# A two-part kernel (complex scan and local attention) on one core: engines of some stores and evictions, and a new recording order

## The chip, the core and the metric

The kernel runs on one core of one Trainium2 chip. The time is the device time of a run in microseconds (us); where several runs are given, the median counts. Engines are named as in the profile: PE (TensorE, matmuls), PEld (its weight loads), DVE (VectorE), ACT (ScalarE), POOL (GpSimd) and SP (SyncE, which here only begins DMAs). SPq and ACTq stand for the issue of DMAs in the queues of SP and ACT.

## The reference

Two independent computations share one output of 1 x 2048 x 896 in bf16: columns 0 to 447 are A's, 448 to 895 are B's. Inputs are bf16, S = 2048, D = 448.

```python
def A(x, Lambda_re, Lambda_im, B_re, B_im, C_re, C_im, log_dt, Dskip):
    Lam = Lambda_re + 1j * Lambda_im                    # 448 complex states
    Lam_bar = exp(exp(log_dt) * Lam)
    Bu = x @ (((Lam_bar - 1) / Lam)[:, None] * (B_re + 1j * B_im)).T
    h[t] = Lam_bar * h[t - 1] + Bu[t]                   # over 2048 steps
    return 2 * real(h @ (C_re + 1j * C_im).T) + x * Dskip

def B(x, wqkv, wo):                                     # 16 heads of 28
    q, k, v = split(x @ wqkv)
    idx = pos[:, None] - 2 * arange(8)                  # 8 earlier places, 2 apart
    logits = sum(q[s] * k[idx[s]]) * 28 ** -0.5, masked where idx < 0
    return (softmax(logits) weighted sum of v[idx]) @ wo
```

## The kernel before

**Units, order, banks.** The kernel does not issue instructions directly. Each piece of work is a unit that is added to a planner (`P.add(engine or engines, estimated cost, function, dependencies, ...)`), 614 in all. Two tables then fix everything: ORDER lists the units in the order in which they are recorded (an entry x stands for unit x % 1000, on the engine number x // 1000 of its choices), and BANKS gives, in that order, the PSUM bank (of 8; most uses take two neighbours) that each accumulation gets. The costs and priorities in `P.add` are not read in a run; they were used when the tables were made. Each engine then runs its own instructions in the recorded order and waits for semaphores where an operand comes from elsewhere. A unit that is recorded earlier may still have to wait in its engine's queue, and what stands behind it on that engine waits with it.

**B.** `loads` transposes B's x by DMA, in quarters of the first half (b = 0, L349) and four pieces of the second half (b = 1, L353), and loads wqkv by groups of columns (L360, L362). `load_v` (L392) is one unit that issues four loads of the v part, wv (L337 to L341). `prep` projects q and k: `first` (PE L494) takes the first 256 columns of b = 0 in quarters, `proj` (PE L453) the rest; kinds K, Q by groups of 128 columns, and kind M for the last 64 columns of both, whose weights are gathered into `wm` by a copy (u_wm, DVE L434). ACT evicts each accumulation to q and k (L202 CAST for k, L204 ACTIVATE for the scaled q). A matmul of 64 partitions (`rr`) runs in a half-row mode of the PE array. `qk` multiplies q with shifted k on DVE (L560, prods; a half product is 128 x 4 x 512) and sums over the head on PE (L573) into logits. `softmax` evicts the logits (ACT L600, L609), sums and normalizes. The attention weights are copied to the layout that `pv` wants (L202 COPY ra, 128 x 512, by ACT or DVE). `v_proj` (PE L673, L682) projects v; `pv` multiplies weights and shifted v on DVE (L727) and adds in a tree (L733 to L744), block by block (b = 0, then b = 1), transposes by DMA (L771) and multiplies with wo on PE (L790, and the half-row L797). Its evictions (`ev2`) and stores (L807) go out in pairs of rows; the last pair is split by row ("tail").

**A.** `setup` makes the powers of Lam_bar: an exponential (ACT L957), two sines (ACT L960, behind a table load), their squares and products on DVE (L987 to L1002), Gd (L1023). A's x is loaded by DMA transposes (L868, on SP's queue), Bcat by evictions of `setup_weights`. `scan` treats the 448 complex states as 896 rows in seven blocks m0 to m6 of 128: input matmuls (L1135), a local scan over 16 steps with powers (`powers`: one block's pw is built by ACT L1082 in single products, or by DVE L1084 in a wide one), evictions on ACT (eP L1148, e L1156, eG L1163, pbuf L1174 and more) and on PE small matmuls on pbuf and pw (L1179, L1185), until h[m] is evicted (L202 CAST h). Three pad buffers go round, so block m + 3 waits for block m's last eviction, and pw goes round in four. `outputs` multiplies h with Ccat on PE (L1319, two rows of 16 at once: 7 blocks for each), with x times D put in by a matmul or by ACT (`seed`, L1331), evicts (L202 CAST ra) and stores (L1342). The last three of the eight pairs are evicted and stored by row; of the very last row ACT evicts 256 columns and DVE 192.

**Queues.** All 20 stores go out from SP's queue; so do wv's loads and nearly all others.

Of the kernel before, what the change touches and what calls it, by code (L numbers as in the profile page):

```python
# [16 lines left out]
D = 448  # L17
# [58 lines left out]
]  # L76
BANKS = [
# [3 lines left out]
]  # L81
# [8 lines left out]
def act(n):  # L90
    return n / 1200.0 + 0.055
# [6 lines left out]
def vec2(n):  # L98
    return n / 1920.0 + 0.07
# [1382 lines left out]
```

## Time and profile before

| | us |
|---|---|
| median of 3 runs | 135.98 (134.9 to 136.2) |
| the profiled execution's own time | 135.03 |
| its span in the profile | 133.3 |
| PE busy | 126.8 (95% of the span) |
| DVE busy | 113.4 (85%) |
| ACT busy | 105.4 (79%) |
| POOL busy | 12.1 (9%) |

The span runs from the first to the last instruction that the profile shows; the run's own time is 1.7 us longer. A row of the timeline gives the start and the length in us, the engine, the line of the kernel, the operation, the tiles written and read, sizes and counts, and in brackets the idle time ahead of it with what ended it. The granted clock of PE was 1.00 in the stages used below.

### The profile page before, as it was taken

How to read it: one execution, taken by the hardware profiler on the slowest of the kernel's cores; microseconds unless marked ns; L12 is line 12 of the kernel's file. 1: busy time of each engine (PE TensorE's matmuls, PEld its weight loads, DVE VectorE, ACT ScalarE, POOL GpSimd, SP SyncE). 2: the span in 40 equal slices, each digit the busy share in tenths (PEclk: the TensorE clock that was granted, in tenths of full speed). 3: DMA queues.
4: the chain of work that ended last, by engine and by line, in shares of the span. 5: the costliest groups of instructions: out<-in, count | busy, mean ns of one | idle time of the engine just before them, and what ended most of it. 6: DMA issues, size and time to landing. Idle time of an engine off the chain costs nothing.

```text
span 133.3 us, 2479 instructions
## 1 busy us (share of the span) xinstructions
PE 126.8 (95%) x921; PEld 63.4 (48%) x921; DVE 113.4 (85%) x130; ACT 105.4 (79%) x189; POOL 12.1 (9%) x28
## 2 busy tenths in 40 slices
PE   6999989999999999999999899999999999999990
PEld 2477333434546434464454255444566555545430
DVE  5256998999999999999999999999999999992011
ACT  2067968987999957879999999989999649569270
POOL 6940491000000000000000000000000000000000
PEclk9999999999999999999999999999999999999998
DMA  4999949989346758827869988006620685318642
GB/s 91 207 199 186 146 100 232 178 193 201 73 91 104 170 147 290 222 51 152 266 97 143 260 210 244 19 0 138 147 67 0 165 227 199 102 63 219 234 148 93
DMA packets 47759, 20.25 MB, mean 152 GB/s; under 512 B 38774, under 2 KB 46346, under 8 KB 47748
## 3 DMA queue, kind: packets, MB, share of 16 engines
q1 hardware_dynamic: 46676, 19.77, 64.7%
q10 hardware_dynamic: 880, 0.31, 1.2%
q8 instruction: 7, 0.11, 0.4%
q0 software_dynamic: 192, 0.03, 0.1%
q14 instruction: 4, 0.03, 0.1%
HBM read 5.18 MB, written 4.19 MB: 70 GB/s over the span
## 4 chain that ended last, share of the span: by engine, by line
PE 73%; ACT 15%; SPq 5%; DMA 3%; issue 1%; DVE 0%; ACTq 0%
PE banks L1319 16%; PE banks L1135 12%; PE banks L453 10%; PE banks L790 7%; PE banks L673 7%; PE banks L573 6%; SPq L349 4%; PE banks L1179 3%; DMA rb<-in_B_wqkv_dram 3%; ACT qk L202 2%; ACT pbuf L1174 2%; PE banks L1152 2%; ACT h L202 2%; PE banks L797 2%; ACT banks L1217 1%; SPq L360 1%
## 5 line engine op out<-in xcount | busy, mean ns | idle before, releaser
L560 DVE TENSOR_TENSOR prods<-qk 128x4096 bf16<-128x4096 bf16 (+1 forms) x18 | 31.7, 1809 | 0.3 <-ACT qk L202 0.2
L1135 PE MATMUL banks<-xaT_sb,Bcat 128*128 128x512 bf16 (+1 forms) x112 | 26.9, 381 | 0.6 <-ACT h L202 0.6
L202 ACT CAST ra<-banks 128x896 bf16<-128x896 f32 (+2 forms) x24 | 17.9, 773 | 7.8 <-PE banks L797 4.2
L202 ACT CAST qk<-banks 128x512 bf16<-128x512 f32 (+3 forms) x20 | 16.9, 843 | 3.9 <-PE banks L453 1.4
L733 DVE TENSOR_TENSOR prods<-prods 128x7168 bf16<-128x7168 bf16 x4 | 15.6, 3892 | 0.1
L727 DVE TENSOR_TENSOR prods<-ra 128x7168 bf16<-128x7168 bf16 x4 | 15.5, 3886 | 0.0
L727 DVE TENSOR_TENSOR prods<-ra,qk 128x7168 bf16<-128x7168 bf16 x4 | 15.5, 3886 | 0.1
L1319 PE MATMUL banks<-Ccat,h 128*128 128x448 bf16 x64 | 14.7, 353 | 0.0
L453 PE MATMUL banks<-rb 128*128 128x512 bf16 (+1 forms) x64 | 13.3, 379 | 0.6 <-ACT sh L960 0.6
L1135 PEld LDWEIGHTS <-Bcat 128*128 128x128 bf16 (+1 forms) x112 | 9.1, 100 | 9.7 <-issue 3.7
L673 PE MATMUL banks<-wv,rb 128*128 128x448 bf16 (+1 forms) x64 | 13.7, 354 | 0.0
L1319 PE MATMUL banks<-Ccat,qk 128*128 128x448 bf16 x48 | 11.7, 352 | 0.0
L790 PE MATMUL banks<-wo_p,rb 128*128 128x448 bf16 x48 | 10.9, 354 | 0.0
L1174 ACT CAST pbuf<-banks 128x64 bf16<-128x64 f32 (+1 forms) x42 | 9.3, 229 | 0.9 <-PE banks L1179 0.6
L1179 PE MATMUL banks<-pbuf,pw 128*128 128x64 bf16 x77 | 9.7, 235 | 0.2
L204 ACT ACTIVATE qk<-banks 128x512 bf16<-128x512 f32 (+2 forms) x10 | 8.4, 849 | 1.2 <-PE banks L453 1.0
L1179 PEld LDWEIGHTS <-pw 128*128 128x128 bf16 x77 | 6.5, 105 | 5.5 <-issue 1.9
L453 PEld LDWEIGHTS <-rb 128*128 128x128 bf16 (+1 forms) x64 | 5.1, 96 | 7.9 <-issue 2.8
L206 DVE CAST ra<-banks 128x192 bf16<-128x192 f32 x2 | 0.7, 358 | 9.2 <-ACT ra L202 9.2
L1319 PEld LDWEIGHTS <-h 128*128 128x128 bf16 x64 | 5.8, 98 | 5.3 <-issue 0.7
L1084 DVE TENSOR_TENSOR pw<-Dm,spair 128x1280 bf16<-128x1280 bf16 (+1 forms) x13 | 8.0, 664 | 0.0
L1148 ACT CAST eP<-banks 128x1024 bf16<-128x1024 f32 x7 | 7.1, 1014 | 0.9 <-PE banks L1135 0.9
(145 smaller groups left out, 201.8 us busy)
## 6 DMA issues: line engine op xcount, KB each, us to landing
out_dram<-ra SPq DMA_DIRECT2D x12, 224.0 KB, 2.3
xaT_sb<-in_A_x_dram SPq DMA_DIRECT2D x2, 448.0 KB, 4.8
out_dram<-ra SPq DMA_DIRECT2D x8, 112.0 KB, 1.7
ra<-ra SPq DMA_DIRECT2D x2, 392.0 KB, 4.1
qk<-qk SPq DMA_DIRECT2D x2, 392.0 KB, 4.1
wv<-in_B_wqkv_dram SPq DMA_DIRECT2D x2, 336.0 KB, 4.2
ra<-ra SPq DMA_DIRECT2D x1, 588.0 KB
qk<-qk SPq DMA_DIRECT2D x1, 588.0 KB, 5.6
```

The source lines that it names most:

```text
L202: nc.scalar.copy(out, in_)
L204: nc.scalar.mul(out, in_, scale)
L453: nc.tensor.matmul(out(e)[:, j0:j1], lhsT=w, rhs=self.xB[rows, b, j0:j1, c, :], start=e not in begun, stop=True, skip_group_check=True)
L560: V.tensor_tensor(p[:, :, a:a + n], q[:, t0 + a:t0 + a + n].unsqueeze(1).to_broadcast([NCH, 4, n]), bass.AP(k.tensor, k.offset, [k.ap[0], ...
L673: nc.tensor.matmul(box["ps"][:, e, 0:D], lhsT=self.xB[rows, b, jj, c, :], rhs=self.wv[rows, c, :], start=e not in begun, stop=True, skip_g ...
L727: V.tensor_tensor(out.rearrange("p (u i d h) -> p u i d h", u=4, i=4, d=DH), self.attn[b][:, r].rearrange("p (x u i) h -> p x u i h", x=2, ...
L733: V.tensor_tensor(T1, T1, T2, op=ALU.add)
L790: nc.tensor.matmul(ps, lhsT=o[:, kt + x, :], rhs=self.wo_p[:, (KT + 1) * x + kt, :], start=(kt == 0), stop=False, skip_group_check=True)
L1135: mt(ps(i), lhsT=lhsT, rhs=rhs, start=i not in begun, stop=True, **kw)
L1174: nc.scalar.copy(pb[:, dst, PAD:PAD + NCH // d], tot(a, d))
L1179: mt(tot(out, 2), lhsT=L(T * unit * k), rhs=pb[:, src, PAD - sh:PAD - sh + NCH // 2], start=False, stop=True, **kw)
L1319: nc.tensor.matmul(ps, lhsT=self.h[m][:, i, g * NCH:(g + 1) * NCH], rhs=self.Ccat[:, m, :], start=False, stop=(m == NM - 1), skip_group_ch ...
```

## The change

Six things change; all but the fourth come from the tables or are allowed by them.

1. Every store unit may be begun by SP or by ACT. In the new table 19 of 20 stay on SP; the very last store (unit 611) is begun by ACT.
2. `load_v` (unit 134), which already had the choice, is now begun by ACT: `1134`.
3. The copy of wm may be done by DVE or ACT. The table leaves it on DVE.
4. The last row of A's and of B's output is evicted whole by one engine (448 columns, on ACT), where ACT did 256 and DVE 192; two units fewer. The last row of a pair no longer depends on the store of the first.
5. One of the attention copies of the first block moves from ACT to DVE (`1192`). The small powers of block m2 move from DVE to ACT (`344`, `1344`), those of m3 from ACT to DVE (`1378`, `378`).
6. ORDER and BANKS are new throughout. At the end of PE's queue B's last pair of rows was done for both rows together (12 matmuls L790, then 4 half-row ones L797), with two rows of A's output (14 matmuls L1319) behind it; now it is done row by row (6 and 2, twice) and one row of A's output (7 matmuls) is behind it.

```diff
--- before.py
+++ after.py
@@ -44,40 +44,39 @@
 ORDER = [
-    22, 2, 5, 0, 1, 6, 23, 7, 1017, 4, 8, 3, 9, 39, 15, 41, 16, 40, 18, 44, 46, 43, 42, 45, 24, 25, 27, 28, 10,
...
-    210, 171, 1378, 146, 212, 178, 114, 176, 213, 133, 179, 169, 282, 207, 206, 283, 208, 209, 190, 314, 284,
...
-    613,
+    4, 2, 3, 0, 5, 1, 41, 39, 15, 16, 42, 6, 7, 22, 40, 43, 45, 44, 46, 59, 23, 24, 47, 57, 1017, 18, 60, 58,
...
+    154, 157, 98, 86, 97, 130, 163, 99, 125, 84, 165, 120, 108, 122, 111, 1134, 88, 162, 158, 159, 310, 100, 33,
...
+    311, 283, 285, 286, 209, 210, 211, 287, 288, 213, 316, 313, 549, 289, 290, 312, 291, 1192, 292, 314, 318,
...
+    539, 543, 542, 544, 590, 594, 595, 596, 579, 608, 609, 607, 597, 540, 541, 545, 546, 547, 548, 610, 1611,
 ]
 BANKS = [
...
...
 ]
@@ -431,8 +430,8 @@
         self.u_proj = []
         lim = PRI["lim"]
         sc = DH ** -0.5
-        self.u_wm = P.add("DVE", vec2(896), lambda: nc.vector.tensor_copy(
-            self.wm[:], self.wqk.rearrange("p k (a c) -> p k a c", a=2)[:, :, :, DF:D]),
+        self.u_wm = P.add(("DVE", "ACT"), (vec2(896), act(896) + 0.05), lambda eng: cx.copy(
+            eng, self.wm[:], self.wqk.rearrange("p k (a c) -> p k a c", a=2)[:, :, :, DF:D]),
             [self.u_wr, *(u for g in "abc" for u in (self.u_w[g, 0], *self.u_w[g, 1]))], 0)
         lo, hi = slice(0, 64), slice(64, NCH)
 
@@ -803,23 +802,22 @@
                     jb["y"] = cx.yb_ring.get()
                 cx.copy(eng, cx.yb_v[:, jb["y"], e0:e1, c0:c1], jb["ps"][:, e0:e1, c0:c1])
 
-            def out(j0=j0, jb=jb, e0=0, e1=2):
-                nc.sync.dma_start(self.out_b[b][:, j0 + e0:j0 + e1, :], cx.yb_v[:, jb["y"], e0:e1])
+            def out(eng, j0=j0, jb=jb, e0=0, e1=2):
+                (nc.sync if eng == "SP" else nc.scalar).dma_start(self.out_b[b][:, j0 + e0:j0 + e1, :], cx.yb_v[:, jb["y"], e0:e1])
                 if e1 == 2:
                     cx.yb_ring.put(jb["y"])
             pr = PRI["wo"]
             us = [P.add("PE", pe(3, 448), lambda f=mm, e=e: f(e), [trs[g % 2][j0 % 4 // 2], self.u_wo], pr, acq=sl) for e in range(2)]
             us += [P.add("PE", pe(1, 448), rr, us[:], pr, mode="r")]
-            en = ("ACT", "DVE")
+            en, st = ("ACT", "DVE"), (("SP", "ACT"), (0.45, 0.45))
             if tail:
                 v = P.add(en, (act(448), vec(448)), lambda eng, f=ev2: f(eng, e1=1), [us[2], *cx.u_free], pr, acq="yb")
-                o = P.add("SP", 0.45, lambda f=out: f(e1=1), [v], pr, lat=1.1, dma=0.5)
-                w = P.add("ACT", act(D - 192), lambda f=ev2: f("ACT", e0=1, c1=D - 192), [us[2], v], pr)
-                w2 = P.add("DVE", vec(192), lambda f=ev2: f("DVE", e0=1, c0=D - 192), [us[2], v], pr)
-                P.add("SP", 0.45, lambda f=out: f(e0=1), [w, w2, o], pr, rel=(sl, "yb"), lat=1.1, dma=0.5)
+                P.add(*st, lambda eng, f=out: f(eng, e1=1), [v], pr, lat=1.1, dma=0.5)
+                w = P.add(en, (act(448), vec(448)), lambda eng, f=ev2: f(eng, e0=1), [us[2], v], pr, rel=sl)
+                P.add(*st, lambda eng, f=out: f(eng, e0=1), [w], pr, rel="yb", lat=1.1, dma=0.5)
             else:
                 v = P.add(en, (act(896), vec(896)), ev2, us + cx.u_free, pr, rel=sl, acq="yb")
-                P.add("SP", 0.45, out, [v], pr, rel="yb", lat=1.1, dma=1.0)
+                P.add(*st, out, [v], pr, rel="yb", lat=1.1, dma=1.0)
 
 
 class PartA:
@@ -1338,8 +1336,8 @@
                     nc.tensor.matmul(jb["y"][:, jj, NCH * k:c1], lhsT=self.xT[:, j + jj, k, :], start=(k == 0), stop=False,
                                      rhs=self.dg[:].rearrange("p a b -> p (a b)")[:, NCH * k:c1], skip_group_check=True)
 
-            def out(j=j, jb=jb, j0=0, j1=2):
-                nc.sync.dma_start(self.out_a[:, j + j0:j + j1, :], cx.ya_v[:, jb["r"], j0:j1])
+            def out(eng, j=j, jb=jb, j0=0, j1=2):
+                (nc.sync if eng == "SP" else nc.scalar).dma_start(self.out_a[:, j + j0:j + j1, :], cx.ya_v[:, jb["r"], j0:j1])
                 if j1 == 2:
                     cx.ya_ring.put(jb["r"])
             sl = jb["s"] = Slot("B", 1, 0 if j // 4 in PES else 1, 2)
@@ -1361,18 +1359,15 @@
                 us = [P.add("PE", pc, lambda f=y, i=i: f(i), self.u_h + self.u_cc + first, pr, acq=sl) for i in range(2)]
             en = lambda n: (("ACT", "DVE"), (act(n) + 0.13 * (n > 512), vec(n)))
             e = lambda f, **k: (lambda eng: f(eng, **k))
+            st = ("SP", "ACT"), (0.45, 0.45)
             if n < 5:
                 v = P.add(*en(896), e(ev), us + x + cx.u_free, pr - 2, rel=sl, acq="ya")
-                P.add("SP", 0.45, out, [v], pr, rel="ya", lat=1.1, dma=1.0)
+                P.add(*st, out, [v], pr, rel="ya", lat=1.1, dma=1.0)
             else:
                 u = P.add(*en(448), e(ev, j0=0, j1=1), us[:1] + x + cx.u_free, pr - 2, acq="ya")
-                o = P.add("SP", 0.45, lambda f=out: f(j0=0, j1=1), [u], pr, lat=1.1, dma=0.5)
-                if n < 7:
-                    v = [P.add(*en(448), e(ev, j0=1, j1=2), [us[1], u], pr - 2, rel=sl)]
-                else:
-                    v = [P.add("ACT", act(256), lambda f=ev: f("ACT", j0=1, j1=2, c1=256), [us[1], u], pr - 2),
-                         P.add("DVE", vec(192), lambda f=ev: f("DVE", j0=1, j1=2, c0=256), [us[1], u], pr - 2)]
-                P.add("SP", 0.45, lambda f=out: f(j0=1, j1=2), [*v, o], pr, rel=("ya", sl) if n == 7 else "ya", lat=1.1, dma=0.5)
+                P.add(*st, lambda eng, f=out: f(eng, j0=0, j1=1), [u], pr, lat=1.1, dma=0.5)
+                v = [P.add(*en(448), e(ev, j0=1, j1=2), [us[1], u], pr - 2, rel=sl)]
+                P.add(*st, lambda eng, f=out: f(eng, j0=1, j1=2), v, pr, rel="ya", lat=1.1, dma=0.5)
 
 
 @with_exitstack
```

Three places of the new order.

The start, on DVE. Ahead of these rows stand the shift copies of q and k's weights; prods are the half products of q and shifted k, wm the gathered weights, sh the sines, la and ab what is made of them. Before:

```order
L206 COPY rb<-rb 64x8x192
L560 TENSOR_TENSOR prods<-qk 128x4x512 x2
L434 COPY wm<-rb 128x896
L973 RECIPROCAL rden<-den 128x7
L560 TENSOR_TENSOR prods<-qk 128x4x512 x4
L987 TENSOR_TENSOR sh<-sh 128x210
```

Of the change:

```order
L971 RECIPROCAL rden<-den 128x7
L205 COPY rb<-rb 64x8x192
L559 TENSOR_TENSOR prods<-qk 128x4x512
L205 COPY wm<-rb 128x896
L559 TENSOR_TENSOR prods<-qk 128x4x512 x2
L985 TENSOR_TENSOR sh<-sh 128x210
```

The square of the sines (L987, now L985) stood behind six half products and stands behind three; the copy of wm behind one instead of two. On PE the wm matmuls of b = 0 stand ahead of the projections of b = 1, and on SP one A transpose (L868) stands between the first and the other three transposes of B's second half (L353).

The loads of wv and the scan, on ACT. The first rows stand among the evictions of the projections, after the sines (qk is q and k, spair and Bcat belong to A's setup). Of the change:

```order
L201 CAST spair<-sfac 128x420
L201 COPY ra<-ra 128x7x64
L203 ACTIVATE qk<-banks 128x1024 x2
L339 DMA wv<-in_B_wqkv_dram 128x3x448
L340 DMA wv<-in_B_wqkv_dram 64x448
L336 DMA wv<-in_B_wqkv_dram 128x3x448
L337 DMA wv<-in_B_wqkv_dram 64x448
L201 CAST qk<-banks 128x1024
L203 ACTIVATE qk<-banks 128x1024
L980 ACT_TABLE_LOAD
```

The four DMA rows are new on ACT; two evictions of the b = 1 projections, a table load and four more evictions stand behind them. Further on stands the first block of the scan (m0 and the begin of m1), with the logits' second eviction (ex_sb). Before:

```order
L1156 CAST e_702<-banks 128x512
L1148 CAST eP<-banks 128x1024
L1163 CAST eG<-banks 128x384
L600 CAST ex_sb<-banks 128x1024
L1174 CAST pbuf_118<-banks 128x64
L202 COPY ra<-ra 128x512 x2
L1174 CAST pbuf_118<-banks 128x64
L1156 CAST e_775<-banks 128x512
```

Of the change:

```order
L1154 CAST e_699<-banks 128x512
L201 CAST ra<-banks 128x896
L1161 CAST eG<-banks 128x384
L201 CAST ra<-banks 128x896
L1172 CAST pbuf_118<-banks 128x64 x2
L1146 CAST eP<-banks 128x1024
L201 COPY ra<-ra 128x512
L1172 CAST pbuf_118<-banks 128x64
L599 CAST ex_sb<-banks 128x1024
```

Two evictions of v (ra, 896) and one attention copy (ra, 512) now stand ahead of the logits' eviction, the second copy of the pair has left this place, and two pbuf copies have moved ahead of it.

The end, on ACT. ra is here the output rows; 896 is a pair, 448 one row. Before:

```order
L202 CAST ra<-banks 128x448
L202 CAST ra<-banks 128x896
L202 CAST ra<-banks 128x448 x3
L202 CAST ra<-banks 128x896
L202 CAST ra<-banks 128x256
L202 CAST ra<-banks 128x448
L202 CAST ra<-banks 128x256
```

Of the change:

```order
L201 CAST ra<-banks 128x448 x2
L201 CAST ra<-banks 128x896
L1329 CAST banks<-xaT_sb 128x2x448
L201 CAST ra<-banks 128x448 x3
L201 CAST ra<-banks 128x896
L201 CAST ra<-banks 128x448 x3
L1340 DMA out_dram<-ra 128x448
```

The two evictions of 256 columns (with DVE's of 192 beside them) are now whole rows, one x-times-D seed (L1331, now L1329) comes later, and the last row on ACT's queue is the store itself.

56 rows, old and new, of tables (BANKS, ORDER) are left out of this document.

## Prediction

> **What bounds the kernel now.** I read the page first, then busy time by stage, then the few places where the fullest engine waits, then the end.
>
> ```profile
> span 133.3 us, 2479 instructions
> PE 126.8 (95%) x921; PEld 63.4 (48%) x921; DVE 113.4 (85%) x130; ACT 105.4 (79%) x189; POOL 12.1 (9%) x28
> ```
> ```profile
> 17.17:33.70 16.53, 16.53 (x130) 6.41 (x130) 16.00 (x21) 13.84 (x16) 3.37 (x4) 1.00 0.95 179
> 33.70:53.00 19.30, 19.30 (x183) 9.44 (x180) 19.18 (x14) 16.69 (x30) 0.00 (x0) 1.00 0.61 146
> 53.00:75.00 22.00, 21.30 (x155) 10.93 (x154) 21.78 (x14) 20.65 (x46) 0.00 (x0) 1.00 0.73 166
> 75.00:107.00 32.00, 31.84 (x233) 16.96 (x231) 31.73 (x16) 29.55 (x63) 0.00 (x0) 1.00 0.48 120
> ```
> Each of the four stages shows its length, then the busy time of PE, of its weight loads, of DVE, ACT and POOL, the granted clock and the share of the DMA engines. Read across: from 17 to 107 us PE has 88.97 of 89.83 us busy, DVE 88.69, ACT 80.73. No matmul is removed, so the new order can win only what PE waits, plus the two ends. PE has room for little: 133.3 - 126.8 is 6.5 us idle, and most of that lies ahead of its first matmul and behind its last. And whatever frees PE soon meets DVE, which has hardly a gap of its own, or ACT in the scan.
>
> Is a busy PE a full PE? One row says so: 35 output matmuls of 448 columns leave in 6.73 us, 0.192 each, without a gap.
>
> ```profile
> 117.50 6.73 PE banks L1319 x35
> ```
> The Trainium skill ("Perfetto Trace Analysis", Identifying the Most-Contended Engine) calls matmul busy time a bad measure and would judge by the weight loads. By it PE, with weight loads 48% of the span, has headroom, and the sum below would be too small a gain. Here the row decides: the issue is back to back where nothing is waited for.
>
> The two waits that PE's own rows show inside the span:
>
> ```profile
> 8.64 5.25 SPq L353 DMA_TRANSPOSE rb<-in_B_x_dram  x4
> 13.93 4.38 SPq L868 DMA_TRANSPOSE xaT_sb<-in_A_x_dram  x3
> ```
> ```profile
> 17.17 3.30 PE L453 MATMUL banks<-rb 64*128 64x512 bf16 x16 [0.65 <-ACT sh L960]
> 20.31 1.78 PE L453 MATMUL banks<-rb,wm 128*128 128x512 bf16 x8
> 21.93 0.59 PE L453 MATMUL banks<-rb 64*128 64x512 bf16 x4
> 22.45 1.48 PE L573 MATMUL banks<-prods,Zsel 128*32 128x512 bf16 x24
> ```
> ```profile
> rb<-in_B_x_dram SPq DMA_TRANSPOSE x8, 4.4
> ```
> The page blames ACT's sine (L960), which these projections do not read. The first row of the queue gives 5.25 / 4 = 1.31 to an issue, so the fourth L353 transpose goes out at about 8.64 + 3 x 1.31 = 12.6; with the median 4.4 to landing it is there at 17.0, just before 17.17. So PE waits for the second half of B's x.
>
> ```profile
> 73.70 1.03 ACT L202 CAST h<-banks 128x1024 bf16<-128x1024 f32 x1
> ...
> 74.77 0.81 PE L1135 MATMUL banks<-xaT_sb,Bcat 128*128 128x512 bf16 x3 [0.58 <-ACT h L202]
> ```
> Here PE waits for ACT's last eviction of scan block m1, which frees the banks and the pad buffer for block m4. ACT is the late one: in 53 to 75 us it is busy 20.65 of 22.00.
>
> **The change, part by part.** The sum is made against the profiled execution: 135.03 us, a span of 133.3 and 1.7 around it. The median of the three times is 135.98, 0.95 higher; I carry the difference over to the median.
>
> *Start, to 33.7 us.* The matmuls on wm that finish B's first half (the eight at 20.31, which take 21.93 - 20.31 = 1.6) are now ahead of the second half's projections, and need only what is loaded by then. One A transpose is put ahead of three of the four L353 (1.3 us more issue), so the last x lands between 17.0 and 18.3; PE, which was there at 17.17 - 0.65 = 16.5, now comes at about 18.1. The 0.65 goes, to within 0.2; what is late next is DVE.
>
> ```profile
> 12.25 2.36 DVE L560 TENSOR_TENSOR prods<-qk 128x2048 bf16<-128x2048 bf16 x2
> 14.53 0.38 DVE L434 COPY wm<-rb 128x896 bf16<-128x896 bf16 x1
> ...
> 19.46 0.78 DVE L987 TENSOR_TENSOR sh<-sh 128x210 f32<-128x210 f32 x1
> ...
> 22.03 0.63 DVE L1023 TENSOR_TENSOR Gd<-Dm,gs 128x896 bf16<-128x896 bf16 x1
> 22.57 0.37 DVE L1002 TENSOR_TENSOR sfac<-ex,sh 128x210 f32<-128x210 f32 x1
> ```
> ```profile
> 14.14 0.60 ACT L204 ACTIVATE qk<-banks 128x512 bf16<-128x512 f32 x1
> ...
> 16.37 0.66 ACT L960 ACTIVATE sh<-ang,turn 128x105 f32<-128x105 f32 x2
> ```
> DVE now comes to the square of the sines (L987) behind three half products instead of six (one is (14.53 - 12.25) / 2 = 1.14) and the copy of wm: 12.25 + 3 x 1.14 + 0.38 = 16.05. ACT has one eviction of half a microsecond less ahead of the sines and ends them at about 16.5 instead of 16.37 + 0.66 = 17.03. So DVE, which never waited here, waits 0.5. Behind it in its queue stand the sine block (22.03 - 19.46 = 2.6), L1002 (0.37; L1023 now goes last) and three half products (3.4): 22.9. PE's 24 score sums start at 22.45 - 0.65 - 0.1 = 21.7, and their last third, which reads those products, two thirds of 1.48 later, at 22.6 to 22.7: a wait of 0.2 to 0.3, and the next products are as late. I give PE DVE's whole half microsecond: -0.65 + 0.55, so this part comes to -0.1 (from -0.65, nothing given back, to +1.0, the DVE wait given back three times).
>
> *wv's four loads on ACT.*
>
> ```profile
> 0.80 0.99 ACTq L360 DMA_DIRECT2D rb<-in_B_wqkv_dram  x2
> ```
> ```profile
> 26.39 0.58 SPq L340 DMA_DIRECT2D wv<-in_B_wqkv_dram  x1
> 27.03 0.52 SPq L341 DMA_DIRECT2D wv<-in_B_wqkv_dram  x1
> 27.59 0.59 SPq L337 DMA_DIRECT2D wv<-in_B_wqkv_dram  x1
> 28.22 0.49 SPq L338 DMA_DIRECT2D wv<-in_B_wqkv_dram  x1
> ```
> ACT pays 0.99 / 2 = 0.5 for an issue at the start, SP 0.55 for each of these. Four hold ACT's queue 2.2 us; behind them stand six bank evictions of the projections. ACT has the room before 33.7 (13.84 busy of 16.53, 2.7 free), so PE loses 0 to 0.6; I take 0 because the late DVE products cover it. If an issue on a full queue costs what a transpose's does (5.25 / 4 = 1.3), it is 5.2 us: that is the slow rival. A lower end, an issue that hides beside ACT's work, gives nothing more on PE. SP loses 2.2 us of issue, which no wait of PE names.
>
> The Trainium skill ("DMA: Bandwidth & Descriptors", Issuing engines are not separate DMA queues) says that starting DMAs on several engines only saves the issuing sequencer's time, since the same 16 DMA engines move them. By it this edit is worth 2.2 us to SP and a loss of 2.2 to ACT, so it speaks against the change; the sum is the same, the slow rival gets its chance from it.
>
> *ACT in the scan.*
>
> ```profile
> 51.87 1.01 ACT L600 CAST ex_sb<-banks 128x1024 bf16<-128x1024 f32 x1 [0.68 <-PE banks L573]
> 53.05 1.14 ACT L202 COPY ra<-ra 128x512 bf16<-128x512 bf16 x2
> ```
> ```profile
> L1082 ACT ACTIVATE pw<-Dm,sfac 128x64 bf16<-128x64 bf16 x10 | 2.5, 332 | 0.0
> L1174 ACT CAST pbuf<-banks 128x64 bf16<-128x64 f32 (+1 forms) x42 | 9.3, 229 | 0.9 <-PE banks L1179 0.6
> ```
> One block's ten power products on ACT (2.5) change places with another's on DVE: nothing. Between the second logits eviction (L600, 51.87) and m1's last eviction (73.70) ACT now does less. A record overlaps the next by about 0.1 (12.25 + 2.36 against 14.53), so an attention copy costs 1.14 / 2 - 0.1 = 0.47: one goes to DVE, one ahead of L600, one behind 73.70; five pbuf copies (0.229 - 0.1 each) are done earlier or later; one 448-column reseed of m2 (about 0.45, as the eviction below) is later: 2.5 us. L600 itself comes about 1.5 later, since wv's 2.2 have eaten ACT's waits before it. So m1's banks are free 1.0 earlier. PE's wait there is 0.58 by its row, and a few of 0.1 lie just before. The links (pbuf copy, then matmul) remain in turn: I take -0.7, from 0 to -1.0. From 73.7 to 107 ACT then has 1.3 more to do, against 32.00 - 29.55 = 2.4 free in that stage: +0.1, from -0.2 to +0.8.
>
> The copy that moves to DVE is 0.25 there by L434 (896 wide in 0.38) and at most ACT's 0.57 (1.14 / 2). One x-times-D product also goes ahead of the last attention step. With its half microsecond from above DVE is up to 0.9 later, less what gaps it has; its last transposes start at most that much later; PE has one more output pass (7 x 0.192 = 1.3) ahead of them as cover.
>
> *Row-mode switches.*
>
> ```profile
> 124.06 2.43 PE L790 MATMUL banks<-wo_p,rb 128*128 128x448 bf16 x12
> 126.43 0.55 PE L797 MATMUL banks<-wo_p,rb 64*128 64x448 bf16 x4
> ```
> Twelve at 0.192 make 2.30, but L797 starts 126.43 - 124.06 = 2.37 after: a switch between whole and half-row matmuls costs a little under 0.1. The new order counts 55 switches on PE for 53: +0.2.
>
> *The end.*
>
> ```profile
> 129.77 0.37 ACT L202 CAST ra<-banks 128x256 bf16<-128x256 f32 x1 [0.79 <-PE banks L1319]
> 130.18 0.36 DVE L206 CAST ra<-banks 128x192 bf16<-128x192 f32 x1 [1.34 <-ACT ra L202]
> 130.56 0.33 SPq L1342 DMA_DIRECT2D out_dram<-ra  x1
> ```
> ```profile
> out_dram<-ra SPq DMA_DIRECT2D x8, 112.0 KB, 1.7
> ...
> rb<-in_B_wqkv_dram ACTq DMA_DIRECT2D x2, 96.0 KB, 2.3
> ```
> ```profile
> L202 ACT CAST ra<-banks 128x448 bf16<-128x448 f32 x6 | 3.2, 535 | 2.7 <-PE banks L797 2.0 <-PE banks L1319 0.8
> ```
> The two halves do not run side by side: DVE starts when ACT has ended. One eviction of 448 on ACT (0.535) ends at 129.77 + 0.535 = 130.30, and the store leaves ACT's own queue by about 130.35 instead of 130.56: -0.2. Landing of a store begun by ACT is in no row; SP's 1.7 is the nearest, the first loads from ACT's queue (2.3) bound it at +0.6, a gain at -0.1. I take 1.7. Of the 20 stores this is the only one that leaves SP, so "SyncE or ScalarE" changes one instruction.
>
> Sum: -0.1 - 0.7 + 0.1 + 0.2 - 0.2 = **-0.7 us**: 134.3 in the profiled run's terms, 135.3 against the median.
>
> **Rivals.**
> 1. *The scan opens up.* m1 is 1.0 earlier and every later link holds it, ACT's 1.3 more fits in its gaps, and the start keeps its 0.65: -0.65 - 1.0 + 0.2 - 0.2 = -1.65, so 134.3. For it: ACT's shorter stretch. Against: DVE's and ACT's full stages.
> 2. *Nothing but the end.* DVE, 88.69 of 89.83 busy, sets the pace, and PE's gains turn into waits for it: -0.2, so 135.8. The change then does not do what a new order is for.
> 3. *Slower: ACT held by wv's loads.* DMA engines are 0.95 busy in that stage; if each issue takes a transpose's 1.3, ACT is 5.2 us late instead of 2.2. The evictions behind free the banks of B's second half; beyond the 0.6 or so of cover PE stops one for one: 3.0 - 0.6 = +2.4, with the sum's -0.7 about +1.7: 137.7. It decides from about 0.7 us an issue.
>
> **How the numbers follow.** Forecast 0.48, rival 1 0.24, rival 2 0.14, rival 3 0.14. About 1% (1.36 us) is what a measurement of this kernel can tell from no change; the three times differ by that. Faster by over 1%: rival 1 and a fifth of the forecast's spread (0.1): 0.34. Slower by over 1%: rival 3 and a little of the forecast's: 0.15. The same: 0.51. The range takes in the forecast with its bounds and rival 1, and leaves out half of rival 3: 133.8 to 136.9.
>
> **What would show it.** Start: no idle mark at the second half's projections, but one on DVE before L987, of about 0.5. Loads: four wv issues of 0.5 to 0.6 on ACT. Scan: m1's last eviction ends by about 73.5, and no mark of 0.5 before m4's input matmuls. End: one 448 eviction, then ACT's issue within 0.1. The forecast is wrong if PE's marks between 17 and 34 us sum to over 1 us, if ACT's issues are much over 0.6, or if PE waits for the last transposes at the end.

## The result and the profile after

The changed kernel takes **147.79 us** (median of 4 runs, 147.66 to 148.26), the kernel before beside it 135.72 us: a ratio of 1.0902 with a 95% interval of 1.084 to 1.0964. The prediction was 135.3 us and a range to 136.9. It is wrong by 12.5 us, and in sign. All ratios leave out runs more than 1.5% above the fastest of the same kernel; medians and ranges take in every run.

The page of the changed kernel, first lines of its parts 1 and 2:

```profile
span 146.1 us, 2464 instructions
...
PE 129.3 (88%) x914; PEld 63.6 (44%) x921; DVE 113.3 (78%) x129; ACT 104.8 (72%) x188; POOL 10.1 (7%) x28
...
PE   6999999600499999999999999899999999999990
...
ACT  3078986000765999876988999999799967884651
...
PEclk9999999965559999999999999999999999999999
```

ACT and DVE have as much work as before, and PE 2.5 us more. What is new is a hole: PE reads 0 in the ninth and tenth of the 40 slices (3.65 us each), ACT in the eighth to tenth, and the granted clock of PE falls in the hole and is low behind it. Its timeline, ACT and ACT's queue first, then PE, then SP's queue:

```profile
22.95 1.93 ACT L203 ACTIVATE qk<-banks 128x1024 bf16<-128x1024 f32 x2
30.87 0.39 ACTq L339 DMA_DIRECT2D wv<-in_B_wqkv_dram  x1
33.04 0.47 ACTq L340 DMA_DIRECT2D wv<-in_B_wqkv_dram  x1
35.73 0.37 ACTq L336 DMA_DIRECT2D wv<-in_B_wqkv_dram  x1
36.94 0.47 ACTq L337 DMA_DIRECT2D wv<-in_B_wqkv_dram  x1
37.46 1.01 ACT L201 CAST qk<-banks 128x1024 bf16<-128x1024 f32 x1 [12.58 <-DMA xa_rest<-in_A_x_dram]
```
```profile
18.58 4.15 PE L452 MATMUL banks<-rb 128*128 128x512 bf16 x21 [0.45 <-DMA rb<-in_B_x_dram]
38.52 1.44 PE L452 MATMUL banks<-rb 128*128 128x512 bf16 x3 [10.50 <-ACT qk L201]
```
```profile
24.05 10.44 SPq L866 DMA_TRANSPOSE xaT_sb<-in_A_x_dram  x8
34.53 1.23 SPq L861 DMA_TRANSPOSE xa_rest<-in_A_x_dram  x1
```

ACT is done with an eviction at 24.88 and begins the first wv load at 30.87. The idle time of 12.58 us up to the next eviction holds the four issues, 0.37 to 0.47 each and 1.70 together; the rest, 10.9 us, is what stands ahead of and between them. The row names what ended the last wait: the landing of a transpose of A's x on SP's queue, data that wv's loads have nothing to do with. The chain of waits shows the same moment:

```profile
34.53 2.39 DMA xa_rest<-in_A_x_dram
36.92 0.02 issue
36.94 0.47 ACTq L337
...
37.46 1.02 ACT qk L201
```

The transpose xa_rest lands at 36.92, and 0.02 us later ACT begins the last wv load. Why it waits for this one is not in the profile but in the built program. It gives the DMAs of SP and ACT eight completion semaphores in turn, in the order of one list across both queues, and each DMA first waits until the one that used its semaphore before, eight places up, has landed. An extract of that list (place among all DMAs of the program, engine, line, what it moves, its semaphore):

```
33 SP  L866 A transpose  takes semaphore 3
34 SP  L866 A transpose  takes semaphore 4
36 SP  L866 A transpose  takes semaphore 6
38 SP  L861 xa_rest      takes semaphore 0
41 ACT L339 wv           waits for semaphore 3 (place 33)
42 ACT L340 wv           waits for semaphore 4 (place 34)
44 ACT L336 wv           waits for semaphore 6 (place 36)
46 ACT L337 wv           waits for semaphore 0 (place 38)
```

Place 34 shows the same as place 38: begun at 29.30, it lands at 33.02, and its wv load begins at 33.04.

On SP such a wait costs little, since what is eight places up was begun by SP itself long before (7 to 10 us before each wv load in the run a_wv_sp below). On ACT the four loads wait for transposes that SP, at 1.3 us an issue, has not begun when ACT comes to them. The Trainium skill ("DMA: Bandwidth & Descriptors", Anatomy of one DMA — SWDGE (gpsimd) path) says that DMA engines do not wait on semaphores; any such wait is done by the sequencer that issues, ahead of the dispatch. The rows agree: ACT itself stands, with six evictions of the projections behind it, and PE behind those.

Theory 1, then: ACT is held by semaphores that it shares with SP's transposes. Its rivals: theory 2, the prediction's own slow case, in which an issue beside full DMA engines is slow by itself; theory 3, the new order is bad, and the stop only covers it.

### The profile page after: what moved, and what is told of

Its sections match the earlier page's. It is cut to its first block, busy times and chain, and to the rows that moved or that the text cites. A ratio compares the mean times of both kernels' runs of the same rounds, so it can differ in the third digit from the quotient of the medians.

```text
span 146.1 us, 2464 instructions
## 1 busy us (share of the span) xinstructions
PE 129.3 (88%) x914; PEld 63.6 (44%) x921; DVE 113.3 (78%) x129; ACT 104.8 (72%) x188; POOL 10.1 (7%) x28
## 4 chain that ended last, share of the span: by engine, by line
PE 60%; SPq 17%; ACT 12%; DMA 5%; issue 2%; ACTq 0%
PE banks L1317 15%; PE banks L1133 11%; SPq L866 8%; PE banks L672 6%; PE banks L789 6%; PE banks L452 4%; PE banks L572 4%; DMA ra<-in_A_B_im_dram 4%; SPq L348 4%; SPq L352 4%; PE banks L1177 3%; ACT h L201 3%; ACT qk L201 2%; DMA xa_rest<-in_A_x_dram 2%; SPq L359 2%
## 5 line engine op out<-in xcount | busy, mean ns | idle before, releaser
L452 PE MATMUL banks<-rb 128*128 128x512 bf16 (+1 forms) x64 | 15.6, 414 | 11.0 <-ACT qk L201 10.5
L201 ACT CAST ra<-banks 128x896 bf16<-128x896 f32 (+1 forms) x24 | 18.4, 787 | 7.2 <-PE banks L1317 5.0
L452 PEld LDWEIGHTS <-rb 128*128 128x128 bf16 (+1 forms) x64 | 5.6, 103 | 20.6 <-issue 16.6
L1172 ACT CAST pbuf<-banks 128x64 bf16<-128x64 f32 (+1 forms) x42 | 10.0, 240 | 4.1 <-PE banks L1177 3.2
L789 PE MATMUL banks<-wo_p,rb 128*128 128x448 bf16 x48 | 10.9, 355 | 0.0
L672 PEld LDWEIGHTS <-rb 128*128 128x128 bf16 (+1 forms) x64 | 5.1, 99 | 5.6 <-issue 2.0
```

Of the source, the lines that this page charges most:

```text
L201: nc.scalar.copy(out, in_)
L452: nc.tensor.matmul(out(e)[:, j0:j1], lhsT=w, rhs=self.xB[rows, b, j0:j1, c, :], start=e not in begun, stop=True, skip_group_check=True)
L672: nc.tensor.matmul(box["ps"][:, e, 0:D], lhsT=self.xB[rows, b, jj, c, :], rhs=self.wv[rows, c, :], start=e not in begun, stop=True, skip_g ...
L789: nc.tensor.matmul(ps, lhsT=o[:, kt + x, :], rhs=self.wo_p[:, (KT + 1) * x + kt, :], start=(kt == 0), stop=False, skip_group_check=True)
L1172: nc.scalar.copy(pb[:, dst, PAD:PAD + NCH // d], tot(a, d))
```

## The experiments

### wv's loads back on SP, and the loads alone in the kernel before

a_wv_sp is the change with one entry put back; b_wv_act the kernel before with only that entry changed.

```diff
 # a_wv_sp, against the change
-    ..., 111, 1134, 88, ...
+    ..., 111, 134, 88, ...
 # b_wv_act, against the kernel before
-    ..., 88, 134, 95,
+    ..., 88, 1134, 95,
```

> The changed kernel with one entry of ORDER put back: wv's four loads (unit 134) are begun by SP again; everything else is as in the change. Theory 1 (semaphores): the built program gives its DMAs eight completion semaphores in turn, across the queues of SP and ACT, and a DMA waits until the one eight places earlier in the program's list has landed; on ACT the four loads then wait for transposes that SP issues at 28.0, 29.3, 31.9 and 34.5 us, and hold ACT from 24.9 to 37.5. On SP the four wait only for DMAs of their own queue that landed long before. The 12.6 us stop goes whole: 134.5 to 136.0 us, the rest of the change being worth -0.7 by the prediction. Theory 2 (the issue itself, the prediction's slow rival): an issue on ACT beside a full DMA system is slow; the stop goes here too. Theory 3 (the new order is bad by itself, and the stop hides it): over 137.5 us.

> The kernel before with one entry of ORDER changed: wv's four loads are begun by ACT. Nothing else. Theory 1 (semaphores): in this program the four loads stand eight places behind the 4th to 7th of the A transposes that follow q's and k's copies; without the four issues SP begins those at about 30.3, 31.6, 32.9 and 34.2 us and they land 3 to 4 us later. So ACT, free at 28.7, begins the loads at about 33.7, 35, 36.5 and 38, each within 0.2 us of such a landing, is held for 9.7 us, and the kernel takes 143.5 to 146 us. Theory 2 (the issue itself): each issue takes the 1.3 us of a transpose, ACT is held 5.2 us, about 138 to 139.5 us, or as long as in the change (12.6). Theory 3 (the new order is to blame): about 135.7, no loss.

a_wv_sp took 136.34 us (12 runs, 135.75 to 136.84): 1.0047 of before, 1.0018 to 1.0076. So about 11.5 of the 12 us are this one entry. It came out above the upper end expected: the rest of the change is worth +0.6 us, not -0.7.

b_wv_act took 146.41 and 148.38 us (two runs; 1.0866, 1.0767 to 1.0965), a little above the 143.5 to 146 of theory 1. The loads alone bring the loss to a kernel whose order is otherwise the old one: theory 3 falls. Its timeline on ACT, and its chain:

```profile
34.65 0.37 ACTq L340 DMA_DIRECT2D wv<-in_B_wqkv_dram  x1
35.07 0.51 ACTq L341 DMA_DIRECT2D wv<-in_B_wqkv_dram  x1
36.53 0.43 ACTq L337 DMA_DIRECT2D wv<-in_B_wqkv_dram  x1
39.74 0.49 ACTq L338 DMA_DIRECT2D wv<-in_B_wqkv_dram  x1
40.32 0.56 ACT L202 COPY ra<-ra 128x448 bf16<-128x448 bf16 x1 [11.64 <-DMA xaT_sb<-in_A_x_dram]
```
```profile
34.64 5.07 DMA xaT_sb<-in_A_x_dram
39.72 0.02 issue
39.74 0.49 ACTq L338
```

The first three issues were expected at 33.7, 35 and 36.5 from the list alone and came at 34.65, 35.07 and 36.53. The last came 1.7 us later than expected, because the transpose eight places up was begun 0.4 later and took 5.07 us to land instead of 3.8; ACT's issue again follows the landing by 0.02. The issues themselves take 0.37 to 0.51, so theory 2 (1.3 each) falls. Theory 1 stands on these times, which it gave before the runs, and on the landings just ahead of the issues; no run gave ACT's loads semaphores of their own with all else kept.

### The loads elsewhere on ACT, and on POOL

a_wv_early keeps the loads on ACT, four instructions earlier, where the program lists them among SP's transposes. a_wv_pool lets POOL begin them; the program gives POOL's DMAs semaphores of their own.

```diff
 # a_wv_early, against the change
-    ..., 74, 36, 276, ...   111, 1134, 88, ...
+    ..., 74, 1134, 36, 276, ...   111, 88, ...
 # a_wv_pool, against the change
-            q = self.nc.sync if eng == "SP" else self.nc.scalar
+            q = {"SP": self.nc.sync, "ACT": self.nc.scalar, "POOL": self.nc.gpsimd}[eng]
-        self.u_w[2] = self.plan.add(("SP", "ACT"), (2.3, 2.1), go, ...
+        self.u_w[2] = self.plan.add(("SP", "ACT", "POOL"), (2.3, 2.1, 2.1), go, ...
-    1134
+    2134
```

> The changed kernel with wv's loads still begun by ACT, but four of ACT's instructions earlier (behind the eviction that ends at 21.0 us). The program then lists them among SP's transposes, eight places behind B_im's load (lands 22.4), the third transpose of the group begun at 17.5 (lands about 23.6), q's first copy (lands about 25) and the first wv load itself. Theory 1 (semaphores): issues at about 22.4, 23.6, 25.2 and 27, so ACT is held about 6 us, of which 1.5 it waited anyway: 138 to 141 us. Theory 2 (the issue itself): the DMA engines are as busy at this place, so the hold is as long as in the change: 146 to 148 us.

> The changed kernel with wv's loads begun by POOL (GpSimd), whose DMAs have semaphores of their own in the program and wait for loads that landed in the first 5 us. Neither SP nor ACT pays for the issues. Theory 1 (semaphores): no stop on ACT, 134.5 to 136.0 us, within 0.5 of the run with the loads on SP; lower than that by up to 0.5 if SP's 2.2 us mattered. Theory 2 (the issue itself on a full DMA system): POOL may be held, nobody waits for it until v's projection at about 33 us; the same time. Theory 3 (the new order is bad by itself): over 137.5.

a_wv_early took 144.32 and 142.50 us (two runs), between a_wv_sp and the change, as theory 1 has it, though above its 138 to 141. The issues began at 23.69, 26.07, 28.29 and 28.77, each 1.3 to 3.1 us later than expected, since in this run everything on SP stood later and landed later:

```profile
23.92 4.35 DMA qk<-qk
28.27 0.02 issue
28.29 0.44 ACTq L336
...
28.77 0.51 ACTq L337
```

Here the DMA that holds ACT is no transpose but q's copy (begun 23.92, landed 28.27), the one that stands eight places up. So it is the place in the list that counts, not the kind of transfer.

On POOL the four loads go out back to back, though the DMA engines are busier there (a share of 1.08 from 14.2 to 16.9 us, against 0.70 at ACT's issues in the change):

```profile
14.20 0.86 POOL L339 DMA_DIRECT2D wv<-in_B_wqkv_dram  x1
15.06 0.58 POOL L340 DMA_DIRECT2D wv<-in_B_wqkv_dram  x1
15.62 0.78 POOL L336 DMA_DIRECT2D wv<-in_B_wqkv_dram  x1
16.39 0.54 POOL L337 DMA_DIRECT2D wv<-in_B_wqkv_dram  x1
```

No stop on ACT, and the profiled execution took 136.48 us at a granted clock of 1.00, but the five timed runs 139.19 to 140.29, at mean clocks of 0.975 to 0.988. That was not expected, and no trace shows these five. b_wv_pool asked whether the loads on POOL cost something by themselves: the same edit in the kernel before.

> The kernel before with wv's four loads begun by POOL (GpSimd), in an otherwise unchanged order. POOL's DMAs have completion semaphores of their own, so no stop on ACT. Theory A (SP's 2.2 us of issues matter little): 135.3 to 136.3, as before. Theory B (loads begun by POOL cost something that the profiled execution of a_wv_pool, 136.5 us, did not show and its five timed ones, 139.2 to 140.3, did): 138 to 140 us here too.

It took 137.39 to 141.74 us (median 140.24 of 6). The two runs with a mean clock of 1.00, 137.39 and 138.17, give a ratio of 1.0157 (1.0047 to 1.0267); the other four, 139.87 and more, have clocks of 0.987 and 0.988. That is theory B (138 to 140), with its two shortest runs at and below the lower end. The profile, of the run of 139.87 us, shows what is paid:

```profile
20.22 0.86 POOL L340 DMA_DIRECT2D wv<-in_B_wqkv_dram  x1
30.93 0.62 ACT L202 COPY xaT_sb<-xaT_sb 64x512 bf16<-64x512 bf16 x1 [3.89 <-DMA xaT_sb<-in_A_x_dram]
32.63 3.18 PE L453 MATMUL banks<-rb,wm 64*128 64x512 bf16 x8 [2.98 <-ACT qk L202]
```

POOL waits for nothing ahead of these loads and begins them at 20.2, where SP comes to them at 26.4. Beside them A's transposes land later: the one begun at 19.8 takes 8.4 us to land instead of 5.3 in the kernel before, and the wv loads 7.3 to 8.0 instead of 3.8 to 4.2. ACT waits 3.89 us for a transpose and PE 2.98 for ACT, and behind that wait PE's clock is 0.50 until 35.6 us. The rule of the Trainium skill that the prediction quoted ("DMA: Bandwidth & Descriptors", Issuing engines are not separate DMA queues: the same 16 DMA engines, whoever issues) agrees with these landing times.

### The end alone

b_tail_act has the order and banks of before with the new end: whole rows evicted by ACT, the last store on ACT. b_tail_sp leaves the store on SP.

```diff
-    ..., 548, ..., 612, 613,      # two units for the last row of B, two for A's
+    ...,                  1611,   # one each; b_tail_sp: 611
```

> The kernel before, its order and banks kept, with the end of the change alone: the last row of A's and of B's output is evicted by ACT whole (448 columns) instead of 256 by ACT and 192 by DVE, and the very last store is begun by ACT. Theory A (the prediction's term): the time from PE's end to the end of the span falls by 0.2, from 3.55 to 3.35, the kernel takes 0.1 to 0.3 us less than before. Theory B (a store begun by ACT lands later): 0 to +0.6.

> As b_tail_act, but the last store stays with SP. Theory A: one eviction of 448 (0.53) in place of 0.37 and 0.36 in turn with a hand-over between, so 0.1 to 0.2 less than before, and about 0.05 to 0.1 more than b_tail_act, the hand-over from ACT to SP. Theory B (the two evictions were hidden by something else): no difference to before.

135.50 us (1.0005 of before, 0.9961 to 1.0049) and 135.40 us (0.9973, 0.993 to 1.0015): no difference that can be measured, with 0.1 to 0.3 us as the expected gain well inside both intervals. The term stays undecided by the times. The traces decide it. PE's last matmuls and the last store in b_tail_act, then in b_tail_sp, then PE's last in the kernel before, whose last store begins at 130.56:

```profile
129.25 0.73 PE L1315 MATMUL banks<-Ccat,qk 128*128 128x448 bf16 x3
130.58 0.37 ACTq L1338 DMA_DIRECT2D out_dram<-ra  x1
```
```profile
129.91 0.73 PE L1315 MATMUL banks<-Ccat,qk 128*128 128x448 bf16 x3
131.24 0.33 SPq L1338 DMA_DIRECT2D out_dram<-ra  x1
```
```profile
129.00 0.73 PE L1319 MATMUL banks<-Ccat,qk 128*128 128x448 bf16 x3
```

The store begins 0.60 us behind PE's end with ACT and with SP, and 0.83 before; from PE's end to the end of the span it is 3.40 and 3.36 instead of 3.59 (3.59 also in b_wv_act, which has the old end; 3.40 in the change, 3.41 in a_wv_sp). So the 0.2 is there, and the whole row brings it, not the engine of the store.

### What the rest of the change costs

With wv on SP the new order is slower than the old by 0.2 to 0.8%. PE's marks in a_wv_sp:

```profile
19.56 4.15 PE L452 MATMUL banks<-rb 128*128 128x512 bf16 x21 [1.03 <-ACT qk L201]
39.82 1.14 PE L1133 MATMUL banks<-xaT_sb,Bcat 128*128 128x512 bf16 x5 [0.32 <-DMA xaT_sb<-in_A_x_dram]
44.95 0.82 PE L1133 MATMUL banks<-xaT_sb,Bcat 128*128 128x512 bf16 x3 [0.21 <-DMA xaT_sb<-in_A_x_dram]
80.48 0.33 PE L1177 MATMUL banks<-pbuf,pw 128*128 128x64 bf16 x3 [0.25 <-ACT pbuf L1172]
81.39 0.81 PE L1133 MATMUL banks<-xaT_sb,Bcat 128*128 128x512 bf16 x3 [0.16 <-ACT h L201]
```

The start has a wait of 1.03 (before: 0.65), A's x is waited for (before: not at all), and the scan waits 0.41 instead of 0.58. Three runs took these waits away one by one, by moving entries of ORDER: a_sp_x_first puts the A transpose behind B's x again; a_xorder also issues first the eight A transposes that the scan's first input matmuls read (and two pieces of B's x, 11 and 13, change places); a_best also moves an ACT copy that waits for A's B matrix behind two evictions.

```diff
 # a_sp_x_first, against a_wv_sp: unit 123 (an A transpose) from behind 13 to behind 12
 # a_xorder, against a_sp_x_first: SP's units in this order
+    11, 13, 14, 12, 21, 123, 120, 121, 122, 84, 116, 117, 134, 118, 119, 115, 128, 130, 125, 129, 127, 126, 131, 124
 # a_best, against a_xorder: unit 135 (COPY ra, 128x7x64) from ahead of 107 to behind 108
```

> The changed kernel with wv's loads on SP (as in the run a_wv_sp, 136.3 us) and one more entry of ORDER moved: the A transpose that stands between the first and the other three transposes of B's second half goes behind them again. Theory A (the last transpose of B's x is what PE waits for at the start): it is issued 1.3 us earlier, at 12.6, lands at 17.0 to 17.5 instead of 19.4, and PE's wait of 1.03 us ahead of the b = 1 projections falls to under 0.2, since PE comes there at about 18.1; the kernel gains 0.5 to 1.0 us: 135.3 to 135.8. Theory B (what PE wins there it waits for DVE's products later): the wait moves to the score sums between 22 and 28 us and the time stays at 136.1 to 136.5.

> The run a_sp_x_first (wv's loads on SP, B's x ahead of A's; 136.28 us) with the A transposes in another order on SP: the eight that the first input matmuls of the scan read are issued first, the other eight behind them. Theory A (SP's issues are what bounds A's x, and PE's wait of 1.34 us at 39.8 is for a transpose issued ninth): that wait goes, and at most a third of it comes back at the second eight; 135.0 to 135.6 us. Theory B (what is won there, PE waits for DVE later): the same time, 136.1 to 136.5.

> As a_xorder, and on ACT the copy of A's B matrix that waits for the load of its imaginary part (1.18 us) stands behind two evictions of the projections instead of ahead of them. Theory A: PE's wait of 0.68 us for the eviction at 24.0 goes too; with a_xorder's gain 134.2 to 135.2 us, below the kernel before by about 1 us. Theory B (ACT's later work is late by what was moved, and DVE sets the pace): no gain over a_xorder.

They took 136.28, 136.48 and 136.31 us (1.006, 1.0048 and 1.0078 of before; the widest interval is 1.0037 to 1.0119): three times the time of theory B, no gain. Its reason, DVE, does not show, since no wait of PE behind 10 us is for DVE; the wait each one removed came back elsewhere, in the end as a wait for A's x. PE's marks of a_sp_x_first, then of a_best:

```profile
24.02 2.43 PE L452 MATMUL banks<-rb 128*128 128x512 bf16 x11 [0.68 <-ACT qk L203]
39.80 1.15 PE L1133 MATMUL banks<-xaT_sb,Bcat 128*128 128x512 bf16 x5 [1.34 <-DMA xaT_sb<-in_A_x_dram]
```
```profile
44.95 0.82 PE L1133 MATMUL banks<-xaT_sb,Bcat 128*128 128x512 bf16 x3 [1.84 <-DMA xaT_sb<-in_A_x_dram]
```

The 1.03 at the start went as expected; 0.68 and 1.34 stand in its place. With those gone, 1.84 stands at the second eight transposes. What is left as a bound, in the new order, is the landing of A's x: SP issues without a pause from 0.8 to 44 us, and 2.2 us of it are wv's loads.

So the loads should leave SP, but neither to ACT nor so early. a_pool_late and a_pool_mid are a_best with the loads on POOL, behind a two-element sum on POOL that reads something ACT evicts and so sets the time.

```diff
-            q = self.nc.sync if eng == "SP" else self.nc.scalar
+            q = {"SP": self.nc.sync, "ACT": self.nc.scalar, "POOL": self.nc.gpsimd}[eng]
...
-    134
+    2134
...
+            w, s = self.wv[:, 0, 0:2], self.qT[:, 0, HB:HB + 2]       # a_pool_late
+            w, s = self.wv[0:64, 0, 0:2], self.q3[0:64, 0:2]          # a_pool_mid
+            q.tensor_tensor(w, s, s, op=ALU.add)
```

> As a_best (136.3 us), but wv's loads are begun by POOL, behind a two-element sum on POOL that reads what ACT evicts at about 23 us, so that they start at about 24 us and not at 14 as in a_wv_pool. The sum's result is overwritten by the loads. Theory A (in the new order SP's queue is the bound of A's x, and 2.2 us less on it is what the loads were moved for): PE's wait of 1.84 us for the second eight transposes falls below 0.5, and the kernel takes 134.2 to 135.2 us, less than the kernel before (135.4). Theory B (the 16 DMA engines are the bound, whoever begins the loads): the transposes land as late as before, the wait stays over 1 us: 135.8 to 137.

> As a_pool_late, but the sum on POOL reads q's last columns, which ACT evicts at about 20.5 us instead of 23, so that POOL begins wv's loads at about 23 instead of 25.5. Theory A (in a_pool_late wv was too late, and SP's queue is no bound any more): the last wv load lands at about 33.5 instead of 36.0, PE's wait of 2.58 us for it falls below 0.5, no new wait for A's x; 134.2 to 135.0 us. Theory B (the 16 DMA engines are full there and something is always late): the wait moves to another load; 135.2 to 136.5.

a_pool_late: median 135.52 us of 12 runs (before 135.59; ratio 0.9958, 0.9921 to 0.9995), above the 134.2 to 135.2 expected, and from 134.42 to 145.57, two of them over 145; what those two met is open. Its profiled execution, one of the longer ones (137.26), has no wait for A's x any more and a new one:

```profile
36.00 0.54 PE L674 MATMUL banks<-wv,rb 64*128 64x448 bf16 x3 [2.58 <-DMA wv<-in_B_wqkv_dram]
```

a_pool_mid, with the loads begun at 21.06 instead of 25.45, has neither wait, and PE's largest mark behind 10 us is 0.41. It takes **134.96 us** (12 runs, 134.35 to 136.34; before 136.14 beside it): a ratio of 0.9924, 0.9882 to 0.9965. It is faster than both kernels, by about 0.8% of the one before. The median of that kernel itself lay between 135.41 and 136.14 in the sessions of these experiments, so the gain is 0.5 to 1.2 us. In a_pool_late the loads begin when they did in a_best (25.45 and 25.72), only not by SP, and the 1.84 is gone: SP's queue was the bound there.

## Why the prediction was wrong, point by point

**wv's four loads on ACT (the term that failed).** The step was: four issues hold ACT 2.2 us, ACT has 2.7 free before 33.7, so PE loses 0 to 0.6 and the sum takes 0. The slow rival had 5.2 us of ACT's time. The price of an issue was nearly right (0.37 to 0.47 against 0.55). What was missing is the wait ahead of each: ACT's evictions come 12.58 us late, 10.9 of it waits, PE stands 10.50 us, and the entry costs about 11.5 us. What stands behind the loads in ACT's queue was asked (six evictions), but not what the moved loads themselves wait for in their new queue. On SP the wait for the DMA eight places up was hidden by SP's own order; the move made it one between two engines. The rival had the place, the engine and the sign, but the wrong mechanism and less than half of ACT's delay (5.2 of 12.58). Its check, an issue well over 0.6 us, would not have shown the fault: the issues are short and the idle time ahead of them long. The forecast's other sign, PE's marks between 17 and 34 us over 1 us in sum, does point to it: the idle time of 10.50 begins at 28.02.

**The clock.** The loss has a second part that no case priced. Stretches of the change, then one of a_wv_sp (length, then busy PE, its weight loads, DVE, ACT, POOL, granted clock):

```profile
38.52:43.63 5.11, 5.11 (x13) 1.76 (x13) 0.00 (x0) 4.19 (x4) 0.00 (x0) 0.50 0.44 84
38.52:46.74 8.22, 8.22 (x52) 2.82 (x52) 0.69 (x1) 6.11 (x6) 0.00 (x0) 0.69 0.40 80
```
```profile
28.84:34.55 5.71, 5.71 (x52) 2.25 (x51) 5.71 (x6) 4.97 (x5) 0.00 (x0) 1.00 0.88 198
```

Behind 10.5 us without a matmul the granted clock is 0.50 for another 5.11 us, then 1.00 (0.69 over the whole). The same two places of PE's timeline in the change (its other row, at 38.52, is above) and in a_wv_sp:

```profile
46.74 0.55 PE L672 MATMUL banks<-wv,rb 64*128 64x448 bf16 x4
```
```profile
28.84 0.81 PE L452 MATMUL banks<-rb 128*128 128x512 bf16 x3
...
34.55 0.55 PE L672 MATMUL banks<-wv,rb 64*128 64x448 bf16 x4
```

The same 52 matmuls take 8.22 us instead of 5.71: 2.5 us are the slow clock (half of 5.11 is 2.6). At the end of the stop the change stands 38.52 - 28.84 = 9.7 us behind a_wv_sp, at the first matmul on wv 46.74 - 34.55 = 12.2. The rest of the run wins back 0.7 (146.1 - 134.6 = 11.5). The Trainium skill ("TensorE: Matmul & The Clock Gate", Part 1) says that the array falls to half clock after an idle window of about 3.4 us and returns behind a busy one, and that these windows run free of the kernel. The half clock agrees, and so do the lengths: in the traces it lasts 13.65 us here (29.98 to 43.63), 10.24 in b_wv_act, 6.83 in a_wv_early and 3.41 in b_wv_pool, each a multiple of 3.41. A stop of 2.98 us was enough for it in b_wv_pool.

**Start.** Predicted: the 0.65 goes, DVE waits 0.5. Measured without the loads' stop: the wait grew to 1.03 (0.45 in the change itself), for the same transposes. The step that failed is their landing, put at 17.0 to 18.3 with 4.4 from issue to landing. The transpose put ahead took its 1.3 of issue as said, and PE came there at about 18.1 as said (18.13 and 18.53), but the last piece took 4.48 to land in the change and 5.48 in a_wv_sp (18.44 and 19.42), and PE could only go on at 18.58 and 19.56. DVE shows no wait ahead of L985 (the old L987) in a_wv_sp: ACT ended the sines at about the time DVE came. The order of SP's queue, not DVE, is what was late next.

**A's x.** No term of the sum named it: "SP loses 2.2 us of issue, which no wait of PE names" was true of before and false of the new order, where 0.32 and 0.21 us are waited for it, and up to 1.84 once other waits are gone.

**Scan.** Predicted -0.7: PE's wait ahead of m4 falls from 0.58 to 0.25 + 0.16 = 0.41, a gain of 0.17. **Row modes and end.** PE's busy time is 126.7 in a_wv_sp and 126.8 before, so the 0.2 for switches does not show; the end's -0.2 is below what 12 runs tell apart, and the traces show it (3.59 to 3.40 behind PE's end). The sum of all this without the loads, -0.7, was measured as +0.6 (0.2 to 1.0): by PE's marks the scan brought a quarter of its term, and the start (0.38 more) and A's x (0.53) cost what the sum did not hold.

## What to carry to other kernels

Before a DMA is moved to another engine's queue, list what it will wait for there: where completion semaphores are shared in turn, it waits for the landing of a DMA some places up in the list of all queues, and the whole engine stands behind it. Give such a load to an engine with nothing behind it, or begin it only when what stands ahead in the list has landed; and neither too early, since transfers beside it then land later (8.4 us instead of 5.3 here). How early is too early no run shows by itself: 20.2 us cost time in the old order, 21.1 did not in the new. When one wait after another is removed and the time stays, look for the queue that never pauses: here SP's, as a_pool_mid showed when SP was freed of 2.2 us.

## What the runs showed that was not expected

A stop of 10.5 us on PE costs 2.5 us more in slow clock behind it. Loads begun by POOL at 20 us instead of by SP at 26, in the kernel before, cost 1.6% in the two runs at full clock and more in the others, though no row shows an engine that waits for POOL: what waits is ACT, for transposes that land later. With the loads begun at 14 us in the new order the one traced execution (136.48 us) shows no such price, and why the five others took 139.19 to 140.29 is open. Begun by POOL at 21 us, in the order of a_best, they cost nothing.
